# 640-wide rows in SBUF and one DMA transpose a tile, in place of DRAM copies and TensorE transposes, in an attention-and-MLP block

## The chip, the cores and the metric

The kernel runs on one core of one Trainium2 chip. The metric is the device time of one launch in microseconds (us). Engines are named as in the profile: PE is TensorE, PEld its weight load, DVE VectorE, ACT ScalarE, POOL GpSimd, SP SyncE. "SPq" is SP's instruction queue, from which nearly all DMAs are issued.

## What is computed

One transformer block over S = 2048 positions and D = 576 channels, bf16 in and out:

```python
h   = x + attention(layernorm(x)) @ wo       # wqkv: 576 x 1728, wo: 576 x 576
out = h + mlp(layernorm(layernorm(h)))       # w1: 576 x 4608, w2: 4608 x 576, gelu (tanh form), biases b1, b2
# attention: 32 heads of 18 channels; position s looks at s, s-2, ..., s-14 (window 8, dilation 2)
```

## The kernel before

**Tiles.** Positions go in 16 tiles of 128: tile j holds positions 16p + j on partition p. So the keys that tile j needs are those of tiles j, j-2, ..., and, one partition further up, of the tiles past the start. Even tiles and odd tiles do not meet in the attention. `EVEN` is 0, 2, ..., 14 and `ODD` is 1, 3, ..., 15; QKV runs over even tiles first; attention runs in `ATT_ORDER`, from tile 14 down, then from 15 down. `A[0]` is tile 14, `A[1]` is tile 12. Two tiles of that order make a group of `GROUPS`, and the MLP goes group by group.

**Contraction of 576.** PE contracts 128 rows at once, and every matmul on the weights wqkv, wo and w1 is split further into two 64-row halves that run side by side on the array (`phase`, line 217). The 576 channels are four full blocks of 128 (`KF` = 4) and one block of 64 channels. The last block is wanted on both halves of the partitions, since both row halves take it, each for half of the output columns. So each transposed activation has five blocks (`KT` = 5), the fifth with the same 64 channels twice; before, those are channels 512 to 575. Weights of the fifth block lie in `wqh_sb`, `woh_sb`, `w1h_sb`.

**Three ways to a transposed tile.** (1) On PE: `transpose_in` (line 182) makes five 128-column transposes, the fifth from the last 128 columns, and a sixth (line 186) that puts the 64 channels into the other half; for `EVEN[5:]` DVE writes a doubled tail `xn_tail` (line 800), and five do. ACT or DVE copies the result from PSUM. This serves the normalized x of the even tiles (`tr_x`), o of tiles 14 and 12 (`tr_o`), and LN2 of the same tiles (`tr_h`). (2) For odd tiles of x, two at a time: `out_x` stores 576 columns and the last 64 again to DRAM (lines 284, 285), and `in_x` reads them back with a DMA transpose (line 288). (3) For all later o and LN2: `dma_out` stores one tile to a DRAM buffer `td` in the same two pieces (lines 193, 194), and a DMA transpose reads it (`dma_tr_o`, `read_o`, `ln2_in`).

**Stages.** QKV is 24 visits (`visit`) of two (tile, q/k/v) products each, taken from `seq`. After each, lists `after` and `loads` give what DVE, ACT and SP do next; `between` and `hooks` put work inside a visit; `wo_with` adds the output projection of tiles 14 and 12 to visits 17 and 19. During QKV, DVE already runs the attention of the first tiles: `att_qk_a` multiplies q with the ring of eight key tiles, `att_pv_a` and `att_pv_b` form o (line 401). After a tile's product its slot in the ring is replaced by the rows shifted by one partition, read back from DRAM (`halo`, line 339); those rows were stored by `store_halo` (line 298). The MLP of group k then runs on PE (`mlp1`, then `mlp2`), while DVE and ACT prepare attention and LN2 of later groups.

**Order.** Everything stands under a manual schedule: each engine executes its instructions in the order of the code. SP too: a DMA that must wait for data holds back all later ones on SP. DMAs also take eight completion semaphores in turn, so one waits for the eighth before it. The loads of the weights w1 and w2 are tied to ACT's evacuations (`pace`).

Of the kernel before, what the change touches and what calls it, by code (L numbers as in the profile page):

```python
# [17 lines left out]
def kernel(  # L18
# [13 lines left out]
    P = 128  # L32
# [79 lines left out]
    def load_wqkv(t, k0=0, k1=KF):  # L112
        load(wq_sb[:, k0:k1, t * D:(t + 1) * D],
             A_wqkv[k0 * P:k1 * P, t * D:(t + 1) * D].rearrange("(k p) c -> p k c", p=P))

    def load_wqkv_half(engine, t, r):
        c0 = t * D + r * HALF
        engine.dma_start(out=wqh_sb[half_rows(r), t, :], in_=A_wqkv[KF * P:D, c0:c0 + HALF])

    def load_wo(qs):  # L120
        src = A_wo.rearrange("(h d) c -> h d c", h=H)
        for q in qs:
            load(wo_sb[q * H:(q + 1) * H, :, :], src[:, q:4 * KF:4, :])
            load(woh_sb[q * H:(q + 1) * H, :], src[:, 4 * KF + q % 2, q // 2 * HALF:(q // 2 + 1) * HALF])

    def load_w1h():
        load(b1_bf[:], B_b1.rearrange("(ft p) -> ft p", p=P))
        src = B_w1[KF * P:D, :].rearrange("p (u g c) -> p u g c", u=NU, g=2)
        for r in range(2):
            load(w1h_sb[half_rows(r), :].rearrange("p (u c) -> p u c", u=NU), src[:, :, r, :])  # L130

    def load_w1(c):
        cols = slice(c * F // 6, (c + 1) * F // 6)
        load(w1_sb[:, :, cols], B_w1[0:KF * P, cols].rearrange("(k p) c -> p k c", p=P))
# [7 lines left out]
    def ln_stats(srcs, tag, c1, c0, bufs, first=None, eps=True):  # L142
        n = len(srcs)
        pool = qp if tag.startswith("ln1") else sb
        stats = pool.tile([P, n, 2, nc.vector.BN_STATS_DIM], F32, tag=f"{tag}_stats", name=f"{tag}_stats", bufs=bufs)
# [32 lines left out]
    def transpose_in(pt, src, tail=None):  # L178
        for kt in range(KT):
            c = min(kt * P, D - P)  # L180
            if kt < KF or tail is None:
                nc.tensor.transpose(pt[:, kt, :], src[:, c:c + P], ident[:])  # L182
        if tail is not None:
            nc.tensor.transpose(pt[:, KF, :], tail[:].rearrange("p r c -> p (r c)"), ident[:])
            return
        nc.tensor.transpose(pt[0:HP, KF, :], src[:, KF * P:D], ident[:])


    stored = [None]

    def dma_out(src):
        td = dram.tile([P, KT * P], BF16, tag="td", name="td", bufs=4)
        nc.sync.dma_start(out=td[:, 0:D], in_=src)
        stored[0] = nc.sync.dma_start(out=td[:, D:KT * P], in_=src[:, KF * P:D]).ins
        return td

    def dma_transpose(dst, src):
        td = dma_out(src)
        nc.sync.dma_start_transpose(out=dst, in_=td[:])
# [9 lines left out]

    def phase(duo, swap, after):  # L210
        first = last = None
        n = len(duo["g"][0])
        for i in range(n):
            for kt in range(KF if swap else KT):
                for r in range(2):
                    lhsT, rhs = duo["op"](r ^ swap, i, half_rows(r), kt)
# [36 lines left out]
    xnT, xn_tail = {}, {}  # L253
# [7 lines left out]
    def tr_x(js, tag):  # L261
        pair = psum_pair(tag or "CAB"[(ring_pos[0] + 1) % 3], "xt_pt", BF16)
        for n, j in enumerate(js):
            transpose_in(tr_view(pair, n), q_all[:, j, :], xn_tail.pop(j, None))
# [12 lines left out]
    xd = [dram.tile([2, P, KT * P], BF16, name=f"xd{i}") for i in range(NT // 4)]  # L277

    def odd_x(i):
        return q_all[:, 4 * i + 1:4 * i + 4:2, :]  # L280

    def out_x(i):
        dst = xd[i][:, :, :].rearrange("j p c -> p j c")
        nc.sync.dma_start(out=dst[:, :, 0:D], in_=odd_x(i))
        nc.sync.dma_start(out=dst[:, :, D:KT * P], in_=odd_x(i)[:, :, KF * P:D])

    def in_x(i):
        nc.sync.dma_start_transpose(out=new_xnT(ODD[2 * i:2 * i + 2])[:],
                                    in_=xd[i][:, :, :].rearrange("j p c -> (j p) c"))
# [10 lines left out]
    def qkv_duo(j, t):  # L300
        def make():
# [3 lines left out]
            def op(g, i, sl, kt):  # L305
                c0 = t * D + g * HALF
                return xt[sl, kt, :], (wq_sb[sl, kt, c0:c0 + HALF] if kt < KF else wqh_sb[sl, t, :])
# [90 lines left out]
    def att_pv_b(j):  # L398
        for n in (4, 2):
            nc.vector.tensor_tensor(out=prod[:, 0:n, :], in0=prod[:, 0:n, :], in1=prod[:, n:2 * n, :], op=ALU.add)  # L400
        nc.vector.tensor_tensor(out=q_all[:, j, :], in0=prod[:, 0, :], in1=prod[:, 1, :], op=ALU.add)
# [6 lines left out]
    oT, hn, hnT, h_of = {}, {}, {}, {}  # L408
# [5 lines left out]
    def new_oT(j):  # L414
        oT[j] = sb.tile([P, KT, P], BF16, tag="oT", name="oT", bufs=3)
        return oT[j]

    def tr_o(j, tag):
        pt = tr_view(psum_pair(tag, "o_pt", BF16), 0)
        transpose_in(pt, q_all[:, j, :])  # L420
        nc.scalar.copy(out=new_oT(j)[:], in_=pt)

    def dma_tr_o(j):
        dma_transpose(new_oT(j)[:], q_all[:, j, :])

    def send_o(j):
        o_sent[j] = dma_out(q_all[:, j, :])

    def read_o(j):
        nc.sync.dma_start_transpose(out=new_oT(j)[:], in_=o_sent.pop(j)[:])  # L430

    pw_of, o_sent = {}, {}

    def wo_duo(j, tag):
        def make():
# [3 lines left out]
            def op(g, i, sl, kt):  # L439
                c0 = g * HALF  # L440
                return t[sl, kt, :], (wo_sb[sl, kt, c0:c0 + HALF] if kt < KF else woh_sb[sl, :])
# [29 lines left out]
    def ln2_act(j):  # L471
        h = h_of[j]
        y = sb.tile([P, D], BF16, tag="hn", name="hn", bufs=2)
        nmean, var, rstd = (sb.tile([P, 1], F32, tag=f"ln2_{t}", name=f"ln2_{t}", bufs=2) for t in ("nmean", "var", "rstd"))
        nc.scalar.activation(out=y[:], in_=h[:], func=ACT.Identity, scale=-1.0 / D, accum_out=nmean[:])
        nc.scalar.activation(out=y[:], in_=h[:], func=ACT.Square, bias=nmean[:], accum_out=var[:])
# [4 lines left out]
    def ln2_send(j):  # L481
        h, rstd, nmean, y = hn[j]
        nc.scalar.activation(out=nmean[:], in_=nmean[:], func=ACT.Identity, scale=rstd[:])
        ln_apply_act(y[:], h[:], rstd[:], nmean[:])
        hn[j] = dma_out(y[:])

    def ln2_out(j):
        hn[j] = dma_out(hn[j][:])
# [3 lines left out]
    def ln2_in(j):  # L492
        read[0] = nc.sync.dma_start_transpose(out=hnT_slot(j), in_=hn.pop(j)[:]).ins
        if stored[0] is not None:
            tc.add_manual_dep(read[0], stored[0].name, sync_dep, reason="stores ahead of the transposes of LN2")
            stored[0] = None
# [19 lines left out]
    def ln2_hn(j):  # L516
        h, rstd, nmr = hn[j]
        hn[j] = sb.tile([P, D], BF16, tag="hn", name="hn", bufs=2)
        ln_apply_act(hn[j][:], h[:], rstd[:, 0:1], nmr[:, 0:1])
# [6 lines left out]

    def tr_h(j, tag):
        pt = tr_view(psum_pair(tag, "h_pt", BF16), 0)
        transpose_in(pt, hn.pop(j)[:])
        nc.scalar.copy(out=hnT_slot(j), in_=pt)  # L530
# [11 lines left out]
    def mlp1_duo(grp, us, tag):  # L542
        def make():
# [5 lines left out]
            def op(g, i, sl, kt):  # L549
                f0 = fts[g][i] * P  # L550
                c0 = (GF * us[i // GF] + i % GF) * P
                return (w1_sb[sl, kt, f0:f0 + P] if kt < KF else w1h_sb[sl, c0:c0 + P]), ht[sl, kt, 0:N]
# [198 lines left out]
    with tc.manual_schedule(engines={ENG.PE, ENG.Activation, ENG.DVE, ENG.SP, ENG.Pool}):  # L751
        load_x(EVEN[0:1])
        load_x(EVEN[1:2])
        for r in range(2):
            load_wqkv_half(nc.scalar, 1, r)
        load_wqkv(1, 0, 2)
        load_wqkv(1, 2, KF)
        load_x(EVEN[2:3])
        load_x(EVEN[3:4])
        load_wqkv(2, 0, 2)  # L760
        load_wqkv(2, 2, KF)
# [4 lines left out]
        load_x(ODD[0:4])  # L766
        load_wqkv(0)
        for r in range(2):
            load_wqkv_half(nc.sync, 0, r)
        load_x(ODD[4:8])  # L770
# [24 lines left out]
        def center(j, mean, op):  # L795
            nc.vector.tensor_scalar(out=q_all[:, j, 0:D if j in EVEN[:5] else KF * P],
                                    in0=x_all[:, j, 0:D if j in EVEN[:5] else KF * P], scalar1=mean, scalar2=None, op0=op)
            if j in EVEN[5:]:
                xn_tail[j] = qp.tile([P, 2, HP], BF16, tag="xn_tail", name="xn_tail", bufs=3)
                nc.vector.tensor_scalar(out=xn_tail[j][:], in0=x_all[:, j, KF * P:D].unsqueeze(1).to_broadcast([P, 2, HP]),  # L800
                                        scalar1=mean, scalar2=None, op0=op)
# [35 lines left out]
        def ln1_one(gi, i):  # L837
            j = ln1_groups[gi][i]
            ln_apply(q_all[:, j, :], x_all[:, j, :], ln1[gi][0][:, i, 0:1], ln1[gi][2][:, i:i + 1])

        def ln1_act(gi, i):
            j = ln1_groups[gi][i]
            _, _, rstd, nmr = ln1[gi]
            ln_apply_act(q_all[:, j, :], x_all[:, j, :], rstd[:, i:i + 1], nmr[:, i:i + 1])
# [44 lines left out]
        loads = {v: [c_(load_w1, c)] for c, v in enumerate((3, 4, 9, 13, 15, 17))}  # L889
        for n, v in enumerate((19, 20, 21, 22)):  # L890
# [8 lines left out]
            6: [c_(ln1_rstd, 10), c_(ln1_act, 8, 1), c_(halo, A[0], 1), c_(out_x, 0)],  # L899
            7: [c_(att_qk_rest, A[0], 0), c_(ln1_bias, 10), c_(ln1_act, 8, 2)],  # L900
            8: [c_(att_qk_a, A[1]), c_(att_qk_rest, A[1], 1), c_(ln1_act, 8, 3), c_(in_x, 0), c_(out_x, 1)],
            9: [c_(halo, A[1], 1), c_(ln1_act, 9, 0)],
            10: [c_(att_pv, A[0]), c_(ln1_act, 9, 1), c_(in_x, 1)],
            11: [c_(out_x, 2)],
            12: [c_(ln1_act, 10, 0), c_(halo, A[0], 2)],
            13: [c_(ln1_act, 10, 1), c_(in_x, 2)],
            14: [c_(att_pv, A[1]), c_(out_x, 3)],
            15: [c_(halo, A[1], 2)],
            16: [c_(in_x, 3)],
# [183 lines left out]
```

## Time and profile before

| what | value |
|---|---|
| runs | 363.95, 364.3, 365.63 us; median 364.3 |
| the profiled execution, first to last instruction (the time that the profile has of it) | 364.9 us, granted PE clock 1.000 |
| QKV, to the first matmul of the MLP | 71.05 us |
| DMA packets | 61907, of which 31888 under 512 bytes; 43.70 MB |
| DMA transposes | 4 of x (two tiles each), 14 of o, 14 of LN2 |
| transposes on PE | even tiles of x, and two tiles each of o and of LN2 |

In lines of a timeline the columns are start, length (of all instructions merged in the line), engine, source line, operation, output<-input, count, and in brackets the idle time before it with what ended it. For DMA issues, the length on SP is that of the issuing; the time to landing is given separately. "A <- B: 2.2, 1, 2.2" says that A waited for B, with total, number of times and longest.

### The profile page before, as it was taken

The numbers are of one execution on the slowest core, as the hardware profiler recorded it, in microseconds if no ns is written. First come the engines' busy times: TensorE is split into PE (matmuls) and PEld (weight loads), VectorE is DVE, ScalarE is ACT, GpSimd is POOL, SyncE is SP. The second block draws the span as 40 slices with busy tenths as digits, with TensorE's granted clock in tenths as the row PEclk, the third lists the DMA queues.
The fourth block names the chain that finished last, engine by engine and source line by source line (L and its number), as shares of the span: only waits on it lengthen the run. The fifth ranks groups of instructions, "written<-read, shape, count | busy, mean of one in ns | idle before, by whom it ended". The sixth has DMA issues, their size and how long they took to land.

```text
span 364.9 us, 11410 instructions
## 1 busy us (share of the span) xinstructions
PE 357.1 (98%) x4891; PEld 291.4 (80%) x4891; DVE 302.3 (83%) x422; ACT 229.2 (63%) x507; POOL 37.1 (10%) x47
## 2 busy tenths in 40 slices
PE   8999799999999999999999999999999999999996
PEld 5678687788778878887888778877887788778874
DVE  5899989999899998999899989998799999710431
ACT  4779655799555684468646954695469366805630
POOL 2141003000111020101010211020101100100000
PEclk9999999999999999999999999999999999999999
DMA  7979998984436743531353155503642342120001
GB/s 226 300 153 330 239 238 184 359 286 73 136 103 88 178 178 77 82 110 51 85 121 88 37 131 91 87 35 92 131 64 59 74 84 72 37 56 19 2 2 33
DMA packets 61907, 43.70 MB, mean 120 GB/s; under 512 B 31888, under 2 KB 60176, under 8 KB 61856
## 3 DMA queue, kind: packets, MB, share of 16 engines
q1 hardware_dynamic: 59968, 41.13, 42.2%
q0 software_dynamic: 1728, 1.77, 4.6%
q8 instruction: 38, 0.62, 0.7%
q10 hardware_dynamic: 160, 0.07, 0.1%
q14 instruction: 13, 0.11, 0.1%
HBM read 21.10 MB, written 12.42 MB: 92 GB/s over the span
## 4 chain that ended last, share of the span: by engine, by line
PE 92%; DMA 5%; SPq 1%; ACT 1%; issue 0%; DVE 0%
PE pm L217 38%; PE po L664 26%; PE pq L217 12%; PE po L576 10%; PE pw L217 5%; DMA oT<-td 2%; DMA wq_sb<-in_A_wqkv_dram 1%; DMA xnT<-xd 1%; DMA xd<-q_all 1%; SPq L104 1%; PE xt_pt L182 1%; ACT kv_ring L312 0%; PE h_pt L182 0%; PE o_pt L182 0%; ACT q_all L175 0%
## 5 line engine op out<-in xcount | busy, mean ns | idle before, releaser
L557 ACT ACTIVATE h_all<-pm,b_sb 128x256 f16<-128x256 f32 (+1 forms) x288 | 108.5, 497 | 69.7 <-PE pm L217 69.7
L217 PE MATMUL pm<-hnT,w_sb 64*128 64x256 bf16 x2304 | 143.0, 269 | 0.0
L217 PEld LDWEIGHTS <-w_sb 64*128 64x128 bf16 x2304 | 111.8, 94 | 15.0 <-issue 1.7
L664 PEld LDWEIGHTS <-h_all 128*128 128x128 f16 x512 | 49.4, 98 | 14.0 <-issue 1.6
L217 PE MATMUL pq<-wq_sb,xnT 64*128 64x288 bf16 x768 | 54.7, 283 | 3.1 <-DMA xnT<-xd 2.2
L217 PEld LDWEIGHTS <-xnT 64*128 64x128 bf16 x864 | 43.1, 94 | 13.0 <-DMA xnT<-xd 2.5
L348 DVE TENSOR_TENSOR prod<-prod 128x2304 bf16<-128x2304 bf16 (+1 forms) x64 | 44.2, 691 | 2.0
L394 DVE TENSOR_TENSOR prod<-kv_ring,probs 128x4608 bf16<-128x4608 bf16 x16 | 40.9, 2555 | 2.4 <-DMA kv_ring<-kv_dram 2.0
L342 DVE TENSOR_TENSOR prod<-kv_ring,q_all 128x4608 bf16<-128x4608 bf16 x16 | 40.8, 2549 | 0.5 <-DMA kv_ring<-kv_dram 0.3
L217 PE MATMUL pm<-hnT,w1h_sb 64*128 64x256 bf16 x288 | 39.2, 269 | 0.0
L664 PE MATMUL po<-w2a_sb,h_all 128*128 128x288 bf16 (+1 forms) x282 | 38.9, 286 | 0.0
L400 DVE TENSOR_TENSOR prod<-prod 128x2304 bf16<-128x2304 bf16 (+1 forms) x32 | 33.9, 1058 | 1.1
L576 PEld LDWEIGHTS <-h_all 128*128 128x128 bf16 x288 | 27.9, 98 | 7.9 <-issue 1.0
L664 PEld LDWEIGHTS <-kv_ring 128*128 128x128 f16 x252 | 24.6, 98 | 6.3
L478 POOL TENSOR_TENSOR ln_rstd<-ln_var,mhalf 128x1 f32<-128x1 f32 x13 | 12.0, 924 | 171.1 <-ACT ln_var L477 171.1
L576 PE MATMUL po<-w2a_sb,h_all 128*128 128x288 bf16 x224 | 28.5, 286 | 0.0
L664 PE MATMUL po<-w2b_sb,h_all 128*128 128x288 bf16 (+1 forms) x142 | 21.3, 286 | 0.0
L217 PE MATMUL pw<-wo_sb,oT 64*128 64x288 bf16 x256 | 19.6, 283 | 0.4 <-DMA oT<-td 0.4
L735 ACT COPY po<-po 128x288 f32<-128x288 f32 x18 | 6.9, 384 | 19.7 <-PE po L664 18.6
L644 DVE TENSOR_TENSOR kv_ring<-h_all 128x1536 f16<-128x1536 f16 (+3 forms) x9 | 6.8, 752 | 14.7 <-ACT h_all L557 14.7
L162 POOL TENSOR_TENSOR ln_rstd<-ln_veps,mhalf 128x1 f32<-128x1 f32 (+2 forms) x14 | 13.4, 967 | 50.3 <-DVE ln_veps L156 34.7
L217 PEld LDWEIGHTS <-oT 64*128 64x128 bf16 x288 | 13.6, 94 | 5.0 <-DMA oT<-td 1.2
(110 smaller groups left out, 387.3 us busy)
## 6 DMA issues: line engine op xcount, KB each, us to landing
w_sb<-in_B_w_dram SPq DMA_DIRECT2D x6, 768.0 KB, 5.9
kv_ring<-kv_dram SPq DMA_DIRECT2D x28, 144.0 KB, 2.8
w2a_sb<-in_B_w_dram SPq DMA_DIRECT2D x4, 1008.0 KB, 6.2
kv_dram<-kv_ring SPq DMA_DIRECT2D x13, 288.0 KB, 3.3
out_dram<-o_sb SPq DMA_DIRECT2D x15, 144.0 KB, 2.6
td<-q_all SPq DMA_DIRECT2D x14, 144.0 KB, 1.8
td<-hn SPq DMA_DIRECT2D x14, 144.0 KB, 1.8
x_all<-in_A_x_dram SPq DMA_DIRECT2D x12, 144.0 KB, 2.9
```

The lines of the kernel that those rows point to most:

```text
L162: nc.gpsimd.tensor_tensor(out=rstd[:], in0=veps[:], in1=mhalf[:].to_broadcast([P, n]), op=ALU.pow)
L217: last = nc.tensor.matmul(duo["g"][r ^ swap][i], lhsT=lhsT, rhs=rhs, start=(swap == 0 and i == 0 and kt == 0), stop=(swap == 1 and kt == K ...
L342: nc.vector.tensor_tensor(out=prod[:], in0=k_ring[j % 2], in1=q_all[:, j, :].unsqueeze(1) .to_broadcast([P, W, D]), op=ALU.mult)
L348: nc.vector.tensor_tensor(out=prod[:, :, o * H:o * H + n], in0=prod[:, :, a * H:a * H + n], in1=prod[:, :, c * H:c * H + n], op=ALU.add)
L394: nc.vector.tensor_tensor(out=prod[:].rearrange("p w (d h) -> p w d h", h=H), in0=v_ring[j % 2].rearrange("p w (d h) -> p w d h", h=H), in ...
L400: nc.vector.tensor_tensor(out=prod[:, 0:n, :], in0=prod[:, 0:n, :], in1=prod[:, n:2 * n, :], op=ALU.add)
L478: nc.gpsimd.tensor_tensor(out=rstd[:], in0=var[:], in1=mhalf[:], op=ALU.pow)
L557: pace[0] = nc.scalar.activation(out=hT(grp)[:, f, 0:N], in_=ps[:, r, i * N:(i + 1) * N], func=ACT.Gelu_apprx_tanh, bias=b1_sb[:, f:f + 1] ...
L576: nc.tensor.matmul(banks[half], lhsT=hT(grp)[:, f, i * P:(i + 1) * P], rhs=w2_rows(f)[:, half * HALF:(half + 1) * HALF], start=(f == 0), s ...
L644: nc.vector.tensor_tensor(out=s_slot(t, m0, m1), in0=a, in1=b, op=alu)
L664: nc.tensor.matmul(bank, lhsT=l, rhs=r, start=start, stop=stop, skip_group_check=True)
L735: nc.scalar.copy(out=bank[seed[step][1]], in_=bank[seed[step][0]])
```

## The change

Rows that are to be transposed are 640 wide in SBUF: channels 0 to 319 and then 256 to 575, so channels 256 to 319 stand twice, and block 2 of five is the doubled one (`wide`, `two`, `block`). The engine that computes the row writes it so. One DMA transpose then goes from SBUF to SBUF, with no DRAM copy. Weights are laid out to match: full blocks are rows 0 to 255 and 320 to 575 (`rows_of`), the halved block is rows 256 to 319 (`SHARED`). wqkv, wo and w1 are therefore loaded by row halves; Wo takes twelve DMAs instead of eight, and the order of the first loads of x and wqkv is other. Odd tiles of x are held in the slots of `kv_ring[1]` that their keys and values fill later. o and LN2 share one set of three buffers; `oT` has two instead of three. The even tiles of x stay with PE, with five transposes each. o and LN2 of tiles 14 and 12 go through the DMA transpose too. Places in `after`, `between` and `loads` move with this.

```diff
-    def load_wqkv(t, k0=0, k1=KF):
-        load(wq_sb[:, k0:k1, t * D:(t + 1) * D],
-             A_wqkv[k0 * P:k1 * P, t * D:(t + 1) * D].rearrange("(k p) c -> p k c", p=P))
+    def rows_of(a):
+        return slice(a * (D - 2 * P), a * (D - 2 * P) + 2 * P)
+    SHARED = slice(2 * P, 2 * P + HP)
+    def load_wqkv(t, a):
+        load(wq_sb[:, 2 * a:2 * a + 2, t * D:(t + 1) * D],
+             A_wqkv[rows_of(a), t * D:(t + 1) * D].rearrange("(k p) c -> p k c", p=P))
...
         for q in qs:
-            load(wo_sb[q * H:(q + 1) * H, :, :], src[:, q:4 * KF:4, :])
-            load(woh_sb[q * H:(q + 1) * H, :], src[:, 4 * KF + q % 2, q // 2 * HALF:(q // 2 + 1) * HALF])
+            for a in range(2):
+                d0 = 10 * a + q
+                load(wo_sb[q * H:(q + 1) * H, 2 * a:2 * a + 2, :], src[:, d0:d0 + 5:4, :])
+            load(woh_sb[q * H:(q + 1) * H, :], src[:, 8 + q % 2, q // 2 * HALF:(q // 2 + 1) * HALF])
...
     def load_w1(c):
-        cols = slice(c * F // 6, (c + 1) * F // 6)
-        load(w1_sb[:, :, cols], B_w1[0:KF * P, cols].rearrange("(k p) c -> p k c", p=P))
+        a, cols = c % 2, slice(c // 2 * F // 3, (c // 2 + 1) * F // 3)
+        load(w1_sb[:, 2 * a:2 * a + 2, cols], B_w1[rows_of(a), cols].rearrange("(k p) c -> p k c", p=P))
...
+    WIDE = KT * P
+    def wide(v):
+        return bass.AP(tensor=v.tensor, offset=v.offset, ap=[v.ap[0], [2 * P, 2], [1, WIDE // 2]])
+    def two(v):
+        return v.rearrange("p (a c) -> p a c", a=2)
...
     def dma_transpose(dst, src):
-        td = dma_out(src)
-        nc.sync.dma_start_transpose(out=dst, in_=td[:])
+        return nc.sync.dma_start_transpose(out=dst, in_=src).ins
+    def wide_tile(name):
+        return sb.tile([P, WIDE], BF16, tag="y", name=name, bufs=3)
+    def block(kt):
+        return kt if kt < 2 else 2 if kt == KF else kt + 1
+    def x_wide(j):
+        if j in ODD:
+            return kv_ring[1][:, j // 2, :, :].rearrange("p t d -> p (t d)")[:, 0:WIDE]
+        return q_all[:].rearrange("p j d -> p (j d)")[:, j * D:j * D + WIDE]
...
     def in_x(i):
-        nc.sync.dma_start_transpose(out=new_xnT(ODD[2 * i:2 * i + 2])[:],
-                                    in_=xd[i][:, :, :].rearrange("j p c -> (j p) c"))
+        js = ODD[2 * i:2 * i + 2]
+        new_xnT(js)
+        for j in js:
+            dma_transpose(xnT[j], x_wide(j))
...
-        nc.vector.tensor_tensor(out=q_all[:, j, :], in0=prod[:, 0, :], in1=prod[:, 1, :], op=ALU.add)
+        o_of[j] = wide_tile("o")
+        nc.vector.tensor_tensor(out=two(o_of[j][:]), in0=wide(prod[:, 0, :]), in1=wide(prod[:, 1, :]), op=ALU.add)
...
-        oT[j] = sb.tile([P, KT, P], BF16, tag="oT", name="oT", bufs=3)
+        oT[j] = sb.tile([P, KT, P], BF16, tag="oT", name="oT", bufs=2)
...
     def dma_tr_o(j):
-        dma_transpose(new_oT(j)[:], q_all[:, j, :])
+        dma_transpose(new_oT(j)[:], o_of.pop(j)[:])
...
-        ln_apply_act(y[:], h[:], rstd[:], nmean[:])
-        hn[j] = dma_out(y[:])
+        ln_apply_act(two(y[:]), wide(h[:]), rstd[:], nmean[:])
+        hn[j] = y
...
     def ln2_in(j):
-        read[0] = nc.sync.dma_start_transpose(out=hnT_slot(j), in_=hn.pop(j)[:]).ins
+        read[0] = dma_transpose(hnT_slot(j), hn.pop(j)[:])
...
         load_x(EVEN[0:1])
+        load_wqkv(1, 0)
         load_x(EVEN[1:2])
+        load_wqkv(1, 1)
...
-        load_x(ODD[0:4])
-        load_wqkv(0)
+        load_wqkv(0, 0)
+        load_wqkv(0, 1)
...
+        load_x(ODD[0:4])
         load_x(ODD[4:8])
...
-            nc.vector.tensor_scalar(out=q_all[:, j, 0:D if j in EVEN[:5] else KF * P],
...
+            nc.vector.tensor_scalar(out=two(x_wide(j)), in0=wide(x_all[:, j, :]), scalar1=mean, scalar2=None, op0=op)
...
-        loads = {v: [c_(load_w1, c)] for c, v in enumerate((3, 4, 9, 13, 15, 17))}
-        for n, v in enumerate((19, 20, 21, 22)):
+        loads = {v: [c_(load_w1, c)] for c, v in enumerate((3, 4, 9, 10, 13, 16))}
+        for n, v in enumerate((18, 20, 22, 23)):
...
-            6: [c_(ln1_rstd, 10), c_(ln1_act, 8, 1), c_(halo, A[0], 1), c_(out_x, 0)],
+            6: [c_(ln1_rstd, 10), c_(ln1_act, 8, 1), c_(halo, A[0], 1), c_(in_x, 0)],
...
-            10: [c_(att_pv, A[0]), c_(ln1_act, 9, 1), c_(in_x, 1)],
+            9: [c_(halo, A[1], 1), c_(in_x, 1), c_(ln1_act, 9, 0)],
+            10: [c_(att_den, A[0]), c_(att_pv_a, A[0]), c_(halo, A[0], 2), c_(att_pv_b, A[0]), c_(ln1_act, 9, 1), c_(in_x, 2)],
+            13: [c_(dma_tr_o, A[0])],
+            14: [c_(att_den, A[1]), c_(att_pv_a, A[1]), c_(halo, A[1], 2), c_(att_pv_b, A[1]), c_(in_x, 3)],
+            16: [c_(dma_tr_o, A[1])],
...
-            18: {1: [c_(tr_o, A[1], "D")]},
-            19: [c_(ln2_hn, A[0])],
-            21: [c_(ln2_hn, A[1])],
+            19: [c_(ln2_hn, A[0]), c_(ln2_in, A[0])],
+            21: [c_(ln2_hn, A[1]), c_(ln2_in, A[1])],
...
-            16: c_(tr_o, A[0], "D"),
-            21: c_(tr_h, A[0], "D"),
-            22: c_(tr_h, A[1], "D"),
...
-                m1[0] += [c_(pv_sum, c), c_(send_o, c), c_(pv_sum, d), c_(read_o, c), c_(send_o, d), c_(read_o, d)]
+                m1[0] += [c_(pv_sum, c), c_(dma_tr_o, c), c_(pv_sum, d), c_(dma_tr_o, d)]
```

## The prediction

> **What bounds it now.** I read the page's head first, then TensorE's (PE's) waits, the stretches, and the timelines where a wait stood. The head:
>
> ```profile
> span 364.9 us, 11410 instructions
> ...
> PE 357.1 (98%) x4891; PEld 291.4 (80%) x4891; DVE 302.3 (83%) x422; ACT 229.2 (63%) x507; POOL 37.1 (10%) x47
> ```
>
> PE is the bound at the full granted clock: only fewer PE instructions or fewer PE waits can gain. The median of the runs (364.3) is 0.6 below the profiled span, so nothing outside the span needs pricing, and I subtract what the trace gives from 364.3. 0.5%, about what a measurement of this kernel tells from no change, is 1.8 us. The waits:
>
> ```profile
> PE pq L217 <- DMA xnT<-xd: 2.2, 1, 2.2
> PE pq L217 <- DMA wq_sb<-in_A_wqkv_dram: 0.9, 3, 0.4
> ...
> PE pw L217 <- DMA oT<-td: 0.4, 2, 0.2
> ```
>
> Columns: total us, times, longest. Only 2.2 + 0.4 hang on transposes. By stretch (length, busy PE, PEld, DVE, ACT, POOL with counts, clock, DMA share, GB/s):
>
> ```profile
> 28.20:39.70 11.50, 9.28 (x154) 7.20 (x150) 10.72 (x17) 10.08 (x15) 0.84 (x1) 1.00 0.95 295
> 39.70:71.20 31.50, 31.50 (x497) 25.57 (x499) 28.85 (x41) 19.78 (x34) 3.80 (x2) 1.00 0.94 252
> 71.20:109.30 38.10, 38.10 (x508) 31.34 (x504) 35.91 (x47) 28.30 (x62) 2.25 (x4) 1.00 0.56 160
> ```
>
> The change acts on QKV, up to 71.2: there the DMA engines are at 0.94 to 0.95 and VectorE (DVE) at 0.92 to 0.93, so two other resources stand just behind PE. From 71.2 on PE idles for the 0.4 alone (and the last output).
>
> **Removed from PE.** In the timeline six transposes of a tile (five at L182, one at L186) take 0.39 + 0.17 = 0.56 us. Two tiles of o and two of LN2 go: 4 x 0.56 = 2.24. The odd 64-row transpose goes from five even tiles, 0.17 each; two lie in the start, which waits for weights anyway, so 0.5 counts. The 2.2 wait at 37.5 was for this chain:
>
> ```profile
> 30.46 3.78 DMA xd<-q_all
> ...
> 34.26 0.03 SPq L288
> ...
> 34.32 5.33 DMA xnT<-xd
> ```
>
> Without the store, the two transposes of tiles 1 and 3 are issued where it was, behind the halo at 29.6: about 31 and 32.3 at 1.3 each (the old pair took 1.33 to 1.52 of SP). The first is due at 37.5, six us later; the old pair landed in 3.8 to 5.3. I book the 2.2 as gone. If that cover fails it costs up to 2.2.
>
> **Start.** x of tile 2 now lies behind 288 KB of weights. At the 224 to 323 GB/s of 2 to 6 us that is about 1 us; ACT does its statistics (4.15) ahead of the first copy of xnT, so the first QKV matmul moves from 6.26 to about 7.3. PE waits 0.36 and 0.25 for weights in 6.3 to 9.7, which cover part: +0.5. It cancels the 0.5 above.
>
> **DVE and ACT.** Eight centerings, sixteen sums of o and fourteen LN2 outputs are 640 wide. L401's 576 took 0.46, so 11% is at most 0.05 each; the three separate tails (0.25, some 0.17 net) go. On DVE this cancels, and ACT's 0.1 per LN2 tile is covered by the 15 us of MLP2. Were the two-block operand slow, L401 at double would cost 0.46 a tile, on the path twice.
>
> **Covered.** The load of x of tiles 1 to 7 goes behind Wq: about what stood between them (landings at 13.8 and 16.8) later, and DVE asks for it at 17.7; if it were later than 17.2, DVE would start its chain late by that. W1 by row halves, both wanted before a third is used, is issued by 57 and read from 71. o and LN2 share three buffers and oT has two: each comes back after its reader, two tiles or a group earlier, is through; without that, an oT would wait one landing (3 to 4).
>
> **SP's queue** decides the rest. Loads of Wo become twelve instead of eight, and they stand ahead of the store of K that the first halo needs:
>
> ```profile
> 17.25 0.42 SPq L104 DMA_DIRECT2D woh_sb<-in_A_wo_dram  x1
> ...
> 20.24 0.32 SPq L104 DMA_DIRECT2D wo_sb<-in_A_wo_dram  x1
> ...
> 24.91 0.45 SPq L298 DMA_DIRECT2D kv_dram<-kv_ring  x1
> ...
> 29.59 0.34 SPq L339 DMA_DIRECT2D kv_ring<-kv_dram  x1
> ```
>
> ```profile
> 33.28 2.56 DVE L342 TENSOR_TENSOR prod<-kv_ring,q_all 128x4608 bf16<-128x4608 bf16 x1 [0.27 <-DMA kv_ring<-kv_dram]
> ...
> 46.65 0.46 DVE L401 TENSOR_TENSOR q_all<-prod 128x576 bf16<-128x576 bf16 x1
> ...
> 53.27 0.46 DVE L401 TENSOR_TENSOR q_all<-prod 128x576 bf16<-128x576 bf16 x1
> ```
>
> SP stood until 20.24 for the load of x issued at 11.27 (landing 9.0 us). Then six loads of Wo took 4.1, two of them 0.76 and 1.49. After the change ten follow that wait. At 0.42 each the ten take the same 4.1 (delay 0); four more at 0.42 give 1.7, at the mean of 0.68 give 2.7. I take 0.9, as the long two look like waiting that would shrink. DVE already waits 0.27 for this halo and runs without a gap from 33.28 to 53.7, so the delay passes on: o of tile 14 at 47.1 + 0.9 = 48.0, of tile 12 at 54.6.
>
> **Where the stall goes: Wo.** o was transposed by PE (0.56) and copied by ACT (0.69). Now the DMA does it, issued by SP, and behind each waiting SP instruction the later halos, weights and transposes queue. The source is SBUF, which the trace does not show for a transpose. The nearest rows (us to landing last):
>
> ```profile
> oT<-td SPq DMA_TRANSPOSE x14, 3.8
> ...
> kv_ring<-kv_dram SPq DMA_DIRECT2D x28, 144.0 KB, 2.8
> ...
> x_all<-b_bc SPq DMA_DIRECT2D x12, 144.0 KB, 2.1
> ```
>
> A plain copy from SBUF lands 0.7 sooner than one from DRAM. Single transposes landed in 2.7 to 4.9, the crowded pair in up to 5.3. Bounds: 2.0 (2.7 less 0.7) to 5.3. I take 3.8 for tile 14 and 3.3 for tile 12. Data cost: between 285.4 and 290 only the two transposes of LN2 move, and share times length is 0.09 + 0.73 + 1.47 + 0.19 = 2.5 us for two, so one takes all 16 engines 1.24 us for 160 KB, 132 GB/s.
>
> [...]
>
> Tile 14: SP waits at 45.3 for DVE's PV multiply (halo), issues two transposes of x (to 48.3) and a weight load (0.5), then oT at 48.8; landing 52.6. PE, without its 2.2 and one 0.56, is there at 52.64 - 2.76 = 49.9 and waits 2.7: Wo of tile 14 starts where it did. Tile 12: PE is there 6.18 - 0.56 = 5.6 later, at 58.2. SP: halo at 52.0, two transposes to 55.0, oT lands 58.3. Before, Wo of tile 12 began at 58.82: 0.5 gained of the 3.3 that PE had freed.
>
> **To the MLP.** From there PE has 71.05 - 58.82 less 1.12 for the two LN2 transposes. Tile 12's LN2 output comes from ACT about 5.6 us after Wo ends; its transpose, behind a 1008 KB load of w2a, is due 3.3 later, and single ones landed in 2.8 to 3.5: 0 to 0.7 of wait, I take 0.2. Without that cover it costs what the landing exceeds 3.3. In the first MLP group oT loses its bounce (81.59 to 83.61, 2.0 us), more than DVE's delay; the two late waits go (-0.4).
>
> **Sum:** 0.5 - 0.5 for start and even tiles; 0.5 up to Wo; 1.12 - 0.2 for LN2; 0.4 late: -1.8, so 362.5. Shorter bounces elsewhere, two SP issues and 2 us a tile, lie under the MLP and bring nothing.
>
> **Rivals.** (1) Most of PE's saving stays. If the SP delay is 0 and SBUF transposes land in 2.7, with tile 12's o at 53.7 and no queue ahead, Wo starts at 56.4: -2.4 - 1.12 - 0.4 = -3.9, 360.4. For: no DRAM store stands ahead of a transpose any more. Against: DMA share 0.94. The whole 5.1 cannot come, since PE is at Wo at 55.5 and o is not transposed by then.
> (2) Slower: a transpose reading SBUF occupies the engines or SP longer by e. Three stand in line for each oT, one more for LN2: 4e - 1.8, so it decides from e = 0.45; at double (1.24) it is +3.2, 367.5. For: shares of 0.94 leave no room, twelve transposes now replace four pairs. Against: the SBUF copy landed sooner.
> (3) The change takes its time off PE but the attention on DVE sets the end of QKV anyway: SP delay 1.7 to 2.7, Wo of tile 12 at 59.1 to 60.1, total -1.0 to 0: 363.9. For: DVE has no gap there. Against: part of SP's time was waiting.
>
> **Numbers.** The forecast has 0.50 (own range 361.2 to 364.0, half of it beyond the 0.5%); (1) 0.18, (2) 0.20, (3) 0.12. Faster 0.25 + 0.18 = 0.43; same 0.25 + 0.12 = 0.37; slower 0.20. The range 360.0 to 366.6 leaves out about 0.04 below and 0.12 above.
>
> **What would show it.** No PE wait at 37.5; waits of 2 to 3 us at Wo of tile 14 and little at tile 12; the first MLP matmul near 69.6; the halo load of 29.59 near 30.5. Wrong if Wo waits less than 1 us (rival 1), if oT or xnT lands in over 5 us (rival 2), or if DVE's second QK multiply starts after 35 (rival 3).

## The result: slower, by 1.4%

The changed kernel takes 368.98 us in the median of six runs (368.29 to 372.11), the kernel before 364.58 beside it (363.95 to 365.63): ratio 1.0136, 95% interval 1.0097 to 1.0176. The prediction said 362.5, with 360.0 to 366.6.

The page of the profile after has these lines for those shown of before. The profiled execution is the longest of the six, 3.1 us above their median, so its single stalls are read here and its total is not.

```profile
span 370.3 us, 11302 instructions
...
PE 358.3 (97%) x4862; PEld 292.9 (79%) x4862; DVE 302.9 (82%) x419; ACT 227.5 (61%) x503; POOL 35.3 (10%) x47
...
PEclk9899998989999999999999999999999999999999
```

PE executes 29 instructions less, yet is busy 1.2 us longer: its clock row shows an 8 at three places, all in the first 84 us, where before there was none. Its waits (total us, times, longest):

```profile
PE pw L228 <- DMA oT<-o: 4.4, 2, 4.1
PE pm L228 <- DMA hnT<-hn: 2.0, 1, 2.0
PE xt_pt L196 <- DVE ln_veps L804: 1.4, 1, 1.4
```

The 2.2 us wait for x is gone. In its place stand 4.4 at the two tiles' Wo and 2.0 before the first MLP matmul, both for the new transposes. The same three stretches as before, then the two behind PE's waits (length; busy PE, PEld, DVE, ACT, POOL; clock; DMA share; GB/s):

```profile
28.20:39.70 11.50, 11.50 (x190) 9.28 (x188) 9.67 (x14) 11.40 (x17) 0.85 (x1) 1.00 0.88 266
39.70:71.20 31.50, 27.15 (x415) 21.14 (x412) 25.21 (x39) 15.79 (x27) 3.36 (x2) 0.95 0.92 204
71.20:109.30 38.10, 36.12 (x498) 31.28 (x495) 34.71 (x43) 28.00 (x62) 1.47 (x2) 0.96 0.55 175
...
55.30:59.00 3.70, 3.70 (x34) 2.43 (x36) 0.00 (x0) 1.30 (x2) 0.00 (x0) 0.54 1.14 247
...
76.00:79.50 3.50, 3.50 (x36) 2.99 (x38) 3.25 (x7) 0.45 (x2) 0.00 (x0) 0.51 1.06 367
```

After each of the two waits PE works at about half the granted clock for 3.5 us: the first half of Wo and the product beside it, 2.08 us before (52.64 to 54.72), take 3.77 (55.27 to 59.04). SyncE's issues around the new transposes (start, us of SyncE):

```profile
49.52 0.57 SPq L104 DMA_DIRECT2D w_sb<-in_B_w_dram  x1
50.19 1.20 SPq L199 DMA_TRANSPOSE oT<-o  x1
51.49 0.53 SPq L104 DMA_DIRECT2D w_sb<-in_B_w_dram  x1
...
52.73 3.35 SPq L199 DMA_TRANSPOSE xnT<-kv_ring  x2
56.61 2.04 SPq L199 DMA_TRANSPOSE oT<-o  x1
...
64.21 0.39 SPq L104 DMA_DIRECT2D w2a_sb<-in_B_w_dram  x1
65.69 1.22 SPq L199 DMA_TRANSPOSE hnT<-hn  x1
```

VectorE's second QK multiply and its sums of o, behind the first halo (issued at 30.80 for 29.59):

```profile
34.48 2.56 DVE L345 TENSOR_TENSOR prod<-kv_ring,q_all 128x4608 bf16<-128x4608 bf16 x1 [1.46 <-DMA kv_ring<-kv_dram]
...
47.81 0.49 DVE L405 TENSOR_TENSOR o<-prod 128x640 bf16<-128x640 bf16 x1
...
54.48 0.49 DVE L405 TENSOR_TENSOR o<-prod 128x640 bf16<-128x640 bf16 x1
```

So o is there at 48.3 and 55.0, 1.2 us later than in the first profile of before, and what follows it is late by more. The two oT issued at 50.2 and 56.6 land after 5.0 and 6.2 us, the two hnT of the first tiles after 6.8 and 5.2. The pair of x issued at 52.73, behind the weight load of 51.49, takes 6.7 and 7.0. Over the whole kernel the median of oT and hnT is half of that (us to landing last):

```profile
oT<-o SPq DMA_TRANSPOSE x16, 2.6
hnT<-hn SPq DMA_TRANSPOSE x16, 2.7
```

Before, from DRAM, they were 3.8 and 2.9. So reading SBUF is not slow; the four that hang on PE's path are. Nor does a transpose from SBUF occupy the engines longer: from 289.5 to 292.5 only two of LN2 move, with a DMA share of 0.79, 0.50 and 0.36 in the three microseconds, so one takes 0.8 us of all 16 engines where the prediction worked out 1.24 for one from DRAM.

### The profile page after: what moved, and what is told of

It reads as the page before. It is cut to its first block, busy times and chain, and to the rows that moved or that the text cites. A ratio compares the mean times of both kernels' runs of the same rounds, so it can differ in the third digit from the quotient of the medians.

```text
span 370.3 us, 11302 instructions
## 1 busy us (share of the span) xinstructions
PE 358.3 (97%) x4862; PEld 292.9 (79%) x4862; DVE 302.9 (82%) x419; ACT 227.5 (61%) x503; POOL 35.3 (10%) x47
## 4 chain that ended last, share of the span: by engine, by line
PE 85%; DVE 6%; DMA 5%; SPq 1%; ACT 1%; issue 1%; DVEq 0%
PE pm L228 39%; PE po L646 26%; PE po L558 10%; PE pq L228 5%; PE pw L228 5%; DMA oT<-o 2%; DMA hnT<-hn 1%; DVE prod L345 1%; DVE prod L397 1%; DVE prod L351 1%; DMA x_all<-in_A_x_dram 1%; DMA kv_ring<-kv_dram 1%; SPq L199 1%; PE xt_pt L196 1%; DVE prod L403 1%
## 5 line engine op out<-in xcount | busy, mean ns | idle before, releaser
L228 PE MATMUL pm<-hnT,w_sb 64*128 64x256 bf16 x2304 | 144.7, 271 | 2.0 <-DMA hnT<-hn 2.0
L228 PEld LDWEIGHTS <-w_sb 64*128 64x128 bf16 x2304 | 114.1, 95 | 16.3 <-issue 3.9
L228 PE MATMUL pq<-wq_sb,xnT 64*128 64x288 bf16 x768 | 56.6, 291 | 0.3 <-ACT xnT L283 0.3
L228 PE MATMUL pm<-hnT,w1h_sb 64*128 64x256 bf16 x288 | 40.0, 272 | 0.0
L451 DVE TENSOR_TENSOR h<-pw,x_all 128x576 f32<-128x576 f32 x16 | 11.6, 753 | 8.7 <-PE pw L228 8.6
```

The source lines that it names most:

```text
L228: last = nc.tensor.matmul(duo["g"][r ^ swap][i], lhsT=lhsT, rhs=rhs, start=(swap == 0 and i == 0 and kt == 0), stop=(swap == 1 and kt == K ...
L451: nc.vector.tensor_tensor(out=h[:].rearrange("p (g c) -> p g c", g=2), in0=pw[:, :, 0:HALF], in1=x_of(j).rearrange("p (g c) -> p g c", g=2 ...
```

## Experiments

The theory: the transposes of the first tiles share the 16 DMA engines with weight loads in flight and land 2 to 4 us late; PE waits, and some of its waits are followed by half clock. The rivals: a transpose that reads SBUF is slow by itself; the later start (x of tile 2 behind 288 KB of weights) is to blame; SyncE's order alone is. Ratios are to the kernel before, with 95% intervals. The edits are against the changed kernel and shortened.

**o and LN2 of tiles 14 and 12 back on PE**

```
+ tr_o(j): five transposes into PSUM, ScalarE copy     (16: A[0]; in visit 18: A[1])
- 13: [c_(dma_tr_o, A[0])],   16: [c_(dma_tr_o, A[1])],
+ tr_h(j): the same for hn                             (21: A[0], 22: A[1])
- 19: [..., c_(ln2_in, A[0])],  21: [..., c_(ln2_in, A[1])],
```

> The changed kernel with one part undone: o and the normalised LN2 rows of tiles 14 and 12 are transposed by five PE transposes and one ScalarE copy each, as before the change, instead of one SBUF-to-SBUF DMA transpose each; all else as changed. Theory 'late landing' (the four transposes of the first tiles come back in 5.0, 6.2, 6.8 and 5.2 us and PE waits 4.1, 0.3 and 2.0 us for them): these waits go, PE reaches the visit at 38.7 us still 1.0 us ahead of the kernel before, pays four times five transposes (about 0.45 us a tile by the first xt_pt row, 1.8 us), and the time is 363 to 365 us, 4 to 6 us under the changed kernel's 369.0. Rival 'source in SBUF is slow' (the prediction's second rival): the in_x pairs and the later tiles still pay, so 367 us or more. Rival 'start' (x of tile 2 behind 288 KB of weights): the first pq still starts at 7.5 instead of 6.3 us, and the time stays 1 us or more over 364.6.

364.48 us, ratio 1.0006 (0.9994 to 1.0017): no change against before. PE's waits for oT and hnT are gone, Wo of tile 12 starts at 57.49 instead of 62.89. The whole loss is in this one part. All other SBUF-source transposes are still in the kernel, so the rival of a slow source falls. The later start is still in it too, and costs nothing that can be measured here.

**o alone, LN2 alone**

```
o back on PE:    the tr_o half of the edit above, ln2_in stays
LN2 back on PE:  the tr_h half, dma_tr_o stays
```

> The changed kernel with o of tiles 14 and 12 transposed on PE again; LN2 of these tiles stays with the DMA. If the late landings of o are what costs (waits of 4.1 and 0.3 us at the two visits of Wo, 4.07 us behind the kernel before at the second, and half clock after the first): 4.5 us less what LN2's own landing (2.0 us of wait before the first MLP matmul, half clock after it) keeps: 365 to 366.5 us. If LN2's landing is the larger part: above 366.5.

364.45 us, ratio 1.0007 (0.9988 to 1.0025).

> The changed kernel with LN2 of tiles 14 and 12 transposed on PE again; o of these tiles stays with the DMA. If the late landings of o are the cause, Wo of tile 12 still starts about 4 us late and only the 2.0 us wait before the MLP and the half clock behind it go: 366.5 to 368 us. If both late stages cost alike: near 366.5. If LN2 is the cause: 365 or less.

368.65 us, ratio 1.0121 (1.0095 to 1.0147); PE waits 3.9 us at the first Wo. It is o. With o on PE, LN2's DMA route costs nothing that can be measured: PE waits 1.5 us for a transpose that lands in 4.8, and saves 0.9 us of transposes. With o late, LN2 on PE recovers only 0.3 us, less than the spread of these runs, so the 365 to 366.5 expected of o alone was too high and the loss of o too low.

**Weight loads out of the way, first attempt**

```
- loads of W1 after visits (3, 4, 9, 10, 13, 16), of W2 after (18, 20, 22, 23)
+                          (3, 4, 9, 14, 18, 19),             (22, 22, 23, 23)
```

> The changed kernel with the weight loads taken out from in front of the transposes: thirds of W1 after visits 3, 4, 9, 14, 18, 19 instead of 3, 4, 9, 10, 13, 16, quarters of W2 after visits 22, 22, 23, 23 instead of 18, 20, 22, 23. Theory 'shared DMA queue' (the transposes land late because 768 and 1008 KB loads stand in the same 16 engines): the transposes of o land in about 3 us instead of 5.0 and 6.2, PE's wait at the first Wo falls from 4.1 to about 2 and Wo of tile 12 starts 3 us earlier; the time falls by 2 to 4 us to 365 to 367. Rival 'source in SBUF is slow': landings stay at 5 to 6 us and the time within 0.5 us of 369.0. A later first need of W2 can cost something of its own at the start of the MLP.

374.12 us, ratio 1.0268 (1.0252 to 1.0285): a miss as a time. But its chain holds a pair of landings. The oT issued at 48.2 had no W1 third near it (the last came 6.7 us before); the one at 56.6 came 1.0 us after one:

```profile
48.16 2.65 DMA oT<-o
...
56.55 4.98 DMA oT<-o
```

The pair is a hint and no proof, since the two stand at different places (a DMA share of 0.62 in the one landing, of 1.00 in the other). Wo of tile 14 started at 50.85, 4.4 earlier than in the changed kernel's profile, but at tile 12 PE waited far longer than the 0.26 us there, and the clock was 0.50 from 61.5 to 66.5:

```profile
61.58 1.14 PE L228 MATMUL pw<-wo_sb,oT 64*128 64x288 bf16 x8 [5.04 <-DMA oT<-o]
```

So the MLP starts at 74.97, 1.0 earlier than in the changed kernel's profile. More was lost later: four quarters of W2 in a row held SyncE from 74.2, the halo of a later tile landed 7.4 us after its issue at 85.9, and PE waited 1.9 us at 93.9.

**Weight loads out of the way, second attempt**

```
+ W1 after visits (3, 4, 9, 16, 17, 18), W2 after (20, 21, 22, 23)
```

> The changed kernel with no weight load in front of either transpose of o: thirds of W1 after visits 3, 4, 9, 16, 17, 18 instead of 3, 4, 9, 10, 13, 16, quarters of W2 after visits 20, 21, 22, 23 instead of 18, 20, 22, 23. (In the earlier run with late loads, oT of tile 14 with nothing in front landed in 2.65 us, oT of tile 12 behind one W1 load in 4.98.) Theory 'place in the queue': both land in 2.6 to 3.3 us, PE waits under 1.6 us at each Wo, and Wo of tile 12 starts near 57 us instead of 60 to 63. The time is then 365 to 367 us if the transposes of LN2 still stand behind the loads that moved, which now lie nearer to them. Rival 'source in SBUF is slow or DMA share alone decides': landings stay at 5 us, time 368 or more.

367.91 us, ratio 1.0098 (1.0065 to 1.0130). Both transposes of o now land in time. PE's timeline at the Wo of tiles 14 and 12, and before the MLP (start, us, operation, and the idle time before it in brackets):

```profile
50.65 0.67 PE L228 MATMUL pw<-wo_sb,oT 64*128 64x288 bf16 x8 [1.23 <-DMA oT<-o]
...
57.16 0.66 PE L228 MATMUL pw<-wo_sb,oT 64*128 64x288 bf16 x8 [0.83 <-DMA oT<-o]
...
70.64 0.61 PE L228 MATMUL pm<-hnT,w_sb 64*128 64x256 bf16 x8 [2.41 <-ACT warm L515]
```

From issues at 47.96 and 53.90 that is 2.7 and 3.2 us. The loads now lie beside LN2's transposes, and those land in 7.4 and 5.7. The second, issued at 64.91, comes at 70.6, when PE starts; the row names a ScalarE instruction that ended at the same time, PE's weight loads name the transpose. The delay moved with the loads. Against before, Wo of tile 12 is still about 1 us late (56.13 in the second profile of before, below) although no load stands in its way: SyncE comes to it at 53.9, behind two transposes of x, and the landing takes 3.2 us. This order of loads with LN2 on PE, which would show what o by DMA costs when it lands in time, was not run.

**No load beside LN2's transposes, o on PE**

```
o of tiles 14, 12 on PE; first loads in the order of before; LN2 by DMA
+ W2 after visits (17, 21, 22, 23)
```

> The candidate that the runs point to: of the change, all but two pieces. o of tiles 14 and 12 is transposed on PE and the first loads come in the order of before; LN2 of both tiles goes by SBUF-to-SBUF DMA transposes, and the quarters of W2 are loaded after visits 17, 21, 22, 23 instead of 18, 20, 22, 23, so that no W2 load stands in front of tile 12's LN2 transpose. Theory 'place among the loads': that transpose lands in 2.6 to 3.5 us instead of 4.8 to 7.4, PE waits under 0.5 us for it before the first MLP matmul, and two PE transposes of 0.45 us each are gone against the kernel with o and LN2 on PE (364.0): 363.0 to 363.6, below the kernel before by 0.2 to 0.3%. If the landing stays near 5 us: 364.5 to 366, with PE waiting about 1.5 us.

364.72 us, ratio 1.0008 (0.9990 to 1.0026). Of these two hnT the trace has one landing, that of tile 12's, issued at 64.4:

```profile
DMA to landing us min/median/max: 2.6/2.6/2.6
```

That landing is as expected, 2.6 us, where the hnT of the first tiles took 4.8 to 7.4 beside loads. The gain is not: PE starts the MLP at 68.39, where before it did so at 68.36 (second profile), waits 0.6 us just before it, and 1.1 later at a Wo of the first MLP group. No version beats the kernel before by more than the noise.

**The four transposes on ScalarE's queue**

```
- nc.sync.dma_start_transpose(out=dst, in_=src)
+ (nc.scalar if j in ATT_ORDER[:2] else nc.sync).dma_start_transpose(...)   # o and LN2
```

> The changed kernel with the four transposes of the first tiles (o and LN2 of tiles 14 and 12) issued by ScalarE on its own queue instead of by SyncE; all loads where they were. If the late landing comes from the order in SyncE's queue (they stand behind weights and x of their own queue), they land in 2.6 to 3.5 us here and the time falls to 364 to 366. If it comes from the 16 engines' share (0.9 to 1.3 at these places whoever issues), they still land in 4.5 us or more and the time stays within 1 us of 369.0. Issuing costs ScalarE about 1.2 us each, which lies before its evacuations: up to 0.5 us of PE wait each.

373.57 us, ratio 1.0255 (1.0212 to 1.0298).

```profile
PE pq L228 <- ACT kv_ring L315: 7.9, 4, 6.3
...
oT<-o ACTq DMA_TRANSPOSE x2, 5.8
```

Another queue does not land oT sooner, 5.9 and 5.6 us (hnT 4.7 and 3.9). That fits what is in flight in the shared engines, and not SyncE's order alone. The expected 0.5 us of issue cost was wrong by far. ScalarE is through with its work at 42.5 and o is there at 46.2, but the chain (first line) names the landing of SyncE's pair of x, at 48.2, as what the issue waited for last:

```profile
45.60 2.63 DMA xnT<-kv_ring
...
48.41 1.41 ACTq L199 DMA_TRANSPOSE oT<-o  x1
49.86 0.65 ACT L315 ACTIVATE kv_ring<-pq 128x576 bf16<-128x576 f32 x1 [7.36 <-issue]
```

So ScalarE stands idle for 7.4 us: 3.7 until o is there, 2.0 more until the transposes of the other queue have landed, and 1.4 for the issue. Its evacuations of QKV stand behind that, and PE waits 6.3 us for them. The same with the other order of loads:

> The same with the first loads in the order of before as well: the candidate for beating both kernels. If the landings on ScalarE's queue are under 3.5 us: PE drops 2.2 us of transposes against the kernel with o and LN2 on PE (364.0), o of tile 12 is ready at 52.9 us and lands by 56, near when PE arrives (54.8), so 362.3 to 364. If they land in 4.5 us or more: 367.5 to 368.5, as with that order of loads alone.

373.63 us, ratio 1.0256 (1.0234 to 1.0278), the same stall with 7.4 us at its longest. From 44 to 64 us of the first of the two kernels the transposes of the two queues went one after another: SyncE's next pair of x waited 3.9 us, to 54.44, for the landing of that oT. So here a second queue brought waiting and no overlap.

**Dummy matmuls in PE's gaps**

```
+ fill(6, "B")        before the transposes of x of tile 2
+ 17: {2: fill(18)}   before the first Wo
+ fill(9, "D")        before the first MLP matmul       # 128x512 each, never read
```

> The changed kernel with dummy 128x512 matmuls of a constant (their results are never read) in PE's three gaps: 6 before the transposes of x of tile 2, 18 before the first Wo, 9 before the first MLP matmul. Theory 'clock' (after each of these gaps the granted clock is 0.5 for about 3.5 us, so PE's work there takes nearly twice as long): the clock is 1.00 at 57 to 59 and 77 to 79 us, and since the transposes land no sooner, the time falls by 1.7 us (the stretch after the first MLP matmul) to 3 us, to 366 to 367.3. If the half clock is hidden by the waits that follow: within 0.5 us of 369.0. If the dummies only stretch the gaps: slower than 369.0.

367.59 us, ratio 1.0091 (1.0069 to 1.0113). oT lands in 4.9 and 5.8 us as without them, and the clock is 1.00, in the stretch of the first Wo as over the whole execution:

```profile
53.00:58.00 5.00, 4.94 (x78) 4.31 (x78) 2.22 (x7) 1.69 (x3) 0.14 (x1) 1.00 1.44 224
```

So about 1.4 us of the 4.4 is half clock, which leaves 3.0 to the waits. The two intervals overlap a little, so 1.4 is the best value and not a sharp one.

**Order of the first loads**

```
+ load_x(EVEN[0:1]); load_x(EVEN[1:2]); half rows of K; load_wqkv(1, 0); load_wqkv(1, 1)
```

> The changed kernel with the first loads in the order of before: x of tiles 0 and 2, the half rows of K, then K's two row halves of weights; all else as changed. Theory 'start' (x of tile 2 stands behind 288 KB of weights, first pq 7.49 instead of 6.26 us, then half clock to 12.2): the first pq is back near 6.3 us and the time 1.2 to 1.9 us lower, 367 to 367.8. Theory 'late landing': PE only reaches the first Wo sooner and waits longer for oT there, as SP and DVE set it: the time stays within 0.5 us of 369.0.

368.54 us, ratio 1.0100 (1.0074 to 1.0126): 0.4 us less, within what the intervals allow for none. With o and LN2 on PE as well:

> The changed kernel with o and LN2 of tiles 14 and 12 on PE again and with the first loads in the order of before. With o and LN2 on PE alone the time was 364.5, PE without a wait from 7.4 us to the end but for 0.6. If the later start (first pq at 7.43 instead of 6.26 us) passes to the end, this takes 0.8 to 1.5 us off: 363.0 to 363.7, faster than both kernels. If VectorE's attention chain or SP set the end of QKV: within 0.4 us of 364.5.

363.99 us, ratio 0.9999 (0.9981 to 1.0017): 0.5 below the same kernel with the new order, and level with before. The order costs about half a microsecond, if anything: neither pair is clear of noise.

**The kernel before, profiled again**

> The kernel before, unchanged, profiled a second time. Its first profile has a span of 364.9 us, while its later runs have spans of 362.1 to 363.1, 1.8 to 2.8 us less. If the 2.2 us wait for xnT at 37.5 us stands in every execution, it is here again at 2 us or more with a span near 362.6. If it was an accident of the profiled execution, it is below 1 us here, and the 2.2 us that the prediction booked as gone were not there to be gained.

364.02 us, span 362.2. PE's waits in this execution:

```profile
PE busy L779 <- PEq L1077: 0.8, 1, 0.8
PE pq L217 <- DMA wq_sb<-in_A_wqkv_dram: 0.7, 2, 0.4
PE pw L217 <- DMA oT<-td: 0.5, 2, 0.3
```

There is no wait for xnT. The 2.2 us at 37.5 belonged to an unusual execution: its span of 364.9 lies above the 13 spans of before taken beside the first experiments (362.1 to 363.1), and of the 21 runs beside this one two took over 366 us. Without it PE starts Wo of tile 14 at 49.95, of tile 12 at 56.13 and the MLP at 68.36, each 2.7 us sooner than in the profile that the prediction reckoned from.

## Why the prediction was wrong, step by step

Two terms of the sum failed above all: the wait of 2.2 us that was booked as a gain, and the landing of the transposes before Wo and the MLP. In the profiled execution the misses add up. SyncE issued tile 12's oT at 56.6 for 55.0, it landed in 6.2 us for 3.3, and PE waited 2.0 for 0.2 before the MLP: 6.3 us, and the first MLP matmul came at 75.95 for 69.6. The false start to beat hid another 2.7. Together that is 9.0 of the 9.6 us by which this execution (372.11) missed 362.5; the median missed it by 6.5.

**The 2.2 us booked as gone** were not there in a usual execution. The step that failed is the sentence "the median of the runs (364.3) is 0.6 below the profiled span, so nothing outside the span needs pricing". Every later run has a time 1.7 to 1.9 us above its span (364.02 and 362.2; 372.11 and 370.3). A span of 364.9 therefore belonged to an execution of an estimated 366.7, 2.4 us above the median: the size of that wait. All arrivals of PE were reckoned from it, and so Wo of tile 12 seemed to gain 0.5 where the true start to beat was 56.1 and not 58.8.

**The landing of oT** was taken as 3.8 and 3.3 us, out of bounds of 2.0 to 5.3. It was 5.0 and 6.2 in the profile, 4.9 and 5.8 with the dummies. This is the term that made the change slow: with o back on PE the loss is gone (364.45), and with the loads out of the way two oT landed in 2.7 and 3.2. The row for the upper bound was there, the pair of x at 5.33 in a stretch with a DMA share of 0.95, and the two oT go into just such a stretch; I took values near the median of a landing that is mostly measured in the MLP, where the share is lower: 0.56 from 71.2 to 109.3.

**LN2** was sized at 0.2 us of wait with landings near 3; it was 2.0, with 6.8 and 5.2. The row I leaned on, 2.8 to 3.5 for single transposes, again came from emptier stretches. The 1008 KB load ahead was named and not priced.

**The clock** was not priced at all, since every row of before read 1.00. The waits of 4.1 and 2.0 us were each followed by about 3.5 us at half clock in the profile, and filling the gaps brought 1.4 us in the median. It does not come in every execution: the mean clocks of the six are 0.985 for the profiled one, which has three such stretches (the third at 6.6 to 12.2), 0.991 for two and 0.995 for three. One stretch is worth about 0.005, so by estimate these had two and one.

**SyncE and VectorE** were right in kind and a little small in size. In the twelve profiles with the new loads of Wo the first halo is issued 0.65 to 2.8 us later than in the second profile of before (28.04 against 28.69 to 30.80), 1.3 in the median, for 0.9 predicted, and VectorE's second QK multiply moves from 31.95 to between 32.36 and 34.48. The pairs of x cost SyncE 1.7 us a transpose for 1.3 booked, where the engines are full; 1.26 where they are not. The 640-wide operations cost 0.49 for 0.46. The start was sized at 0.5, and the 0.4 and 0.5 measured for it are not clear of noise.

**The rivals.** The time is nearest to rival 2's 367.5, and its sign in the profile came (oT in over 5 us), but its mechanism did not: the source in SBUF is the faster one, 2.6 against 3.8, and e, the extra occupation of a transpose, is below zero (0.8 us for 1.24). Rival 1 asked for 2.7 us landings without a queue ahead. When a kernel got those (2.7 and 3.2), Wo of tile 12 still started about 1 us later than before, with SyncE's first halo 1.2 us late where rival 1 had no delay. (The "whole 5.1" named there is not the sum of its terms: 2.24, 0.5, 2.2 and 0.4 make 5.3, or 4.8 less the start; nothing rests on it.) Rival 3's chain on VectorE had its delay, but it did not bind: with o and LN2 on PE it has the same delay, and the time is that of before.

**Where to transpose.** With o on PE the kernel takes 364.45 us, with o through the DMA 368.98. Wo of tile 12 came at 62.9, 4.6 later than my 58.3, behind a landing of 6.2; with the engines free the same transpose landed in 2.6. The 132 GB/s gave what one transpose from DRAM occupies, and what mattered was what else was in the engines.

## What to carry to other kernels

A DMA's landing time has to be taken from the stretch where it will run, with the loads in flight there, and not from the median over the kernel: the same 160 KB transpose took 2.6 us with the engines free and, for the first tiles on SyncE's queue beside weight loads, 5.0 and 6.2 in the changed kernel and up to 7.4 in another. Moving a short step from the bound engine to a DMA pays only if input to landing fits before the bound engine arrives; two tiles of o taken off PE saved 0.45 us each and their late landings cost 4.5 net. Before a wait is booked as a gain, look whether the profiled execution is a usual one: compare its span plus the constant outside it with the median, and profile once more if they differ.

## What the runs showed of the hardware

A gap of PE can cost more than its length: with three of them filled the changed kernel took 1.4 us less. After gaps of 3.9 (LN2 on PE), 4.1 (the changed kernel), 4.2 (order of loads), 5.0 (first late loads), 6.3 and 7.4 us (ScalarE's queue) the next matmuls ran at half clock (0.54 after the 4.1, 0.50 after the 4.2), mostly for about 3.5 us and after the 5.0 for 5.0; 1.93 and 1.98 us did so too; after gaps of 2.06, 2.22 and 2.41 us the clock stayed 1.00, and also after 1.5 or less in the middle of a kernel. At the start, 1.4 us (the changed kernel) were followed by a mean clock of 0.70 from 6.6 to 12.2, and after 1.3 us (o and LN2 on PE) the mean of the first 13 us was 0.87; after 1.2 us (LN2 on PE) the first 46 matmuls of QKV took 3.13 us, against 4.80 after the 1.3. So up to 2.4 us length alone does not decide. What does was not tried.

ScalarE's queue stands in order behind a DMA issue that waits: 7.4 us of idle ScalarE, and with it 6.3 us of idle PE, came from one transpose of o put there, which waited for its source and then for transposes of the other queue.
